# Attention ahead of two MoE layers on one core: another order of the attention stage, and fewer weight conversions in it

## The chip, the cores and the metric

The kernel runs on one core of a Trainium2 chip. The metric is device time in microseconds, from a run's start to its end; the median of several runs counts. The engines are TensorE (PE in the profile, its weight loads PEld), VectorE (DVE), ScalarE (ACT), GpSimd (POOL) and SyncE (SP), whose queue issues all transfers.

## The reference

Random-feature attention, then two feed-forward layers, all in float32.

```python
def phi(x):                                    # x scaled by D ** -0.25
    proj = einsum('bhsd,md->bhsm', x, omega)   # D = 64 -> M = 128 features
    h = proj - sum(x * x) / 2
    return exp(h - max(h, axis=-1)) / sqrt(m)
kv  = einsum('bhsm,bhsd->bhmd', phi(k), v)
z   = sum(phi(k), axis=2)
num = einsum('bhsm,bhmd->bhsd', phi(q), kv)
den = einsum('bhsm,bhm->bhs', phi(q), z) + 1e-6
x   = (num / den) as [2304 tokens, 512]
h = x @ w_in;  x = (h - tanh(h)) @ w_out                 # MoE 1, d_ff 2048
h = x @ w_in;  out = (h * sigmoid(1.702 * h)) @ w_out    # MoE 2
```

There are 4 batches of 8 heads, with 576 positions each.

## The kernel before, in words

**Attention.** Two heads (j = 0, 1) form a pair, and there are 16 pairs. The work of a pair is cut into these pieces, each a function:

- `att_a`: q projection on TensorE, features on the partitions (tiles y0, y1 and two of the four hs banks of PSUM).
- `att_a_copy`: ScalarE copies it to pq in SBUF, four copies; after the two of a head, GpSimd takes the maximum over the 128 features (`partition_all_reduce`, L113) into mq.
- `att_sub`, `att_exp`: VectorE subtracts that maximum (L117), ScalarE takes the exponential (L120), once for each head.
- `att_b`: k projection on TensorE, positions on the partitions (two hs banks; the fifth block of positions goes beside the rest of a q projection). `att_b_max`: four VectorE maxima (L143). `att_b_exp`: ten ScalarE exponentials (L148) into kp.
- `att_c`: product of kp and v with 65 columns a head (64 of v, one of ones) on TensorE (L158), into y0 (y2 for pair 0). `att_c_copy`: ScalarE copies it to kvz.
- `att_d`: product of pq and kvz, 65 columns, on TensorE (L175), three blocks into y2 and two into y3. `att_d_norm`: VectorE divides by the last column (L187 to L189), first the three blocks, then the two, into xt.
- `att_e`: transposes on TensorE (L199). `att_e_hi`: ScalarE rounds them to the short format (L213), `att_e_lo`: VectorE takes the rest (L218), and SP writes both to DRAM, from where the MoE reads them; block 0 of the MoE's input is also kept in SBUF.

**Order.** The order on each engine is the order of the program, which is written out by hand in `period(k)`. In steady state a period issues: second normalisation of pair k-2, transposes of k-2, k-v product of k-1, copies of q projection k, subtraction and exponential for head 1 of k-1, bit operations of a conversion, high and low parts of k-2, `kfeat(k)` (k projection, maxima and exponentials, with subtraction and exponential for head 0 of k between), last step of the conversion, q product of k-1 and its first normalisation. The q projection of the next pair opens the next period.

**Weights.** A weight tile (one of 16 per layer) has two halves, input and output weights. Each half comes as 64-bit numbers into one of two raw buffers (`load_w`, 512 KB) and is converted: `conv1` two ScalarE passes (L243, L245), `conv2` two VectorE bit operations (L249, L251), `conv3` a ScalarE cast into the high part (L261), `conv4` the subtraction for the low part (L265), on VectorE during attention and on GpSimd during MoE. Before, the attention stage converts 15 of the 16 half tiles that the first MoE pass wants, one in each period.

**MoE.** 144 steps, in four passes of 36 (two layers, two halves of d_ff each). A step is `h_mm` (12 matmuls, L292), an elementwise chain on ScalarE, VectorE and GpSimd (`elem1`, `elem2`), and `y_mm` (12 matmuls, L339 or L343), which runs three steps behind (LAG). In a pass each block of 512 tokens takes 8 steps, one for each weight tile. `conv_mid` puts conversions behind the elementwise chain: conv1 and conv2 of a new half tile, conv3 and conv4 of the one of the step before; the variable `room` says in which steps. The end of the attention (`tails`) lies between the first three MoE steps.

Of the kernel before, what the change touches and what calls it, by code (L numbers as in the profile page):

```python
# [9 lines left out]
F32 = mybir.dt.float32  # L10
# [8 lines left out]
B, H, S, D, M = 4, 8, 576, 64, 128  # L19
# [4 lines left out]
FP = NF // 2  # L24
# [11 lines left out]
ORDER = ((0, 1, 2, 3, 4), (4, 0, 1, 2, 3), (0, 1, 4, 2, 3), (3, 0, 1, 2, 4))  # L36
LAG = 3
PASSES = ((0, 0), (0, 1), (1, 0))
NWARM = 2


@with_exitstack
def body(ctx, tc, qT, kT, v, om, w1, w2, out):
# [23 lines left out]
    nc.vector.memset(qb, QB)  # L67
    tb = cp.tile([128, 1], F32, name="tb")
    nc.vector.memset(tb, -THR2)
    warm = ap.tile([128, 512], F32, tag="kp", name="warm", bufs=2)  # L70
    nc.vector.memset(warm, 0.0)

    def pt(tag):
        return ps.tile([128, 512], F32, tag=tag, name=tag, bufs=4 if tag == "hs" else 1)
# [31 lines left out]

    def att_a_copy(i, tiles):
        pq = pqs[i] = ap.tile([128, 2, S], F32, tag="pq", name="pq", bufs=2)
        for j in range(2):
            nc.scalar.copy(out=pq[:, j, 0:512], in_=tiles[j])  # L110
            nc.scalar.copy(out=pq[:, j, 512:S], in_=rest[i][j][:, :S - 512])  # L111
            mqs[i, j] = ap.tile([128, S], F32, tag="mq", name="mq", bufs=2)
            nc.gpsimd.partition_all_reduce(  # L113
                mqs[i, j], pq[:, j, :], channels=128, reduce_op=bass.bass_isa.ReduceOp.max)
# [7 lines left out]

    def att_b(i):
        kt = kin.pop(i)
        b, r = (pt("hs"), pt("hs")), rest.pop(i)
        for st in range(ST):
            s0 = min(st * 128, S - 128)
            for j in range(2):
                p = slice(64 * j, 64 * j + 64)
                dst = b[j][:, s0:s0 + 128] if st < 4 else r[j][:, 128:256]  # L130
                nc.tensor.matmul(dst, kt[p, s0:s0 + 128], omd[p, :], start=True, stop=True)  # L131
        kps[i] = ap.tile([128, 2, ST, M], F32, tag="kp", name="kp", bufs=2)
        mx = ap.tile([128, 2 * ST], F32, tag="mx", name="mx", bufs=2)
        return (*b, *r), mx
# [17 lines left out]

    def att_c(i):
        kp, vt = kps.pop(i), vin.pop(i)
        c = pt("y0" if i else "y2")
        for j in range(2):
            for st in range(ST):
                nc.tensor.matmul(  # L158
                    c[:, j * DV:j * DV + DV], kp[:, j, st, :], vt[:, j, st, :], start=(st == 0), stop=(st == ST - 1))
        return c  # L160
# [67 lines left out]
    late = {}  # L228
    NU = 4 * NF

    def load_w(u):
        if u >= NU:
            return
        i, part = divmod(u, 2)
        src = (w1, w2)[i // NF]
        raws[u] = cv.tile([128, 512, 2], I32, tag="raw", name="raw", bufs=2)
        nc.sync.dma_start(
            out=raws[u], in_=src[i % NF, :, part, :].bitcast(I32).rearrange("p (a b) -> p a b", b=2))
# [5 lines left out]
        top = raws[u].bitcast(U16).rearrange("p a (b h) -> p a b h", h=2)[:, :, 0, 1]  # L244
        nc.scalar.activation(out=raws[u][:, :, 0], in_=top, func=AF.Copy, scale=0.9998 * 2.0 ** -13, bias=-0.4995)  # L245

    def conv2(u):
        z, c = raws[u][:, :, 0], raws[u][:, :, 1]
        nc.vector.scalar_tensor_tensor(  # L249
            out=z, in0=c, scalar=-0x80000000, in1=z, op0=ALU.bitwise_and, op1=ALU.bitwise_or)  # L250
        nc.vector.scalar_tensor_tensor(  # L251
            out=c, in0=c, scalar=3, in1=z, op0=ALU.logical_shift_left, op1=ALU.bitwise_or)

# [135 lines left out]

    oms = ap.tile([128, M], F32, name="oms")  # L390
    nc.sync.dma_start(out=oms, in_=om)
    load_q(0)
    load_k(0)
    load_q(1)
    load_v(0)
    load_k(1)
    load_w(0)
    load_w(1)
    omd = ap.tile([128, M], F32, name="omd")
    nc.vector.tensor_scalar(out=omd, in0=oms, scalar1=SCALE, scalar2=None, op0=ALU.mult)  # L400
    ident = ap.tile([128, 128], F32, name="ident")
    make_identity(nc, ident)
    wpt = pt("y3")
    for i in range(NWARM):
        nc.tensor.matmul(wpt, warm[:, :128], warm, start=True, stop=True)
    nc.vector.tensor_copy(out=warm[:, :1], in_=wpt[:, :1])
    new_x((0, 0, 0))


    cu = [0]  # L410
    eparts = {}

    def qexp(i, j):
        att_sub(i, j)
        att_exp(i, j)

    def kfeat(k):
        tiles, mx = att_b(k)
        load_k(k + 2)
        for t in (0, 1):  # L420
            att_b_max(tiles, mx, t)
        if k > 1:
            att_sub(k, 0)
        for t in (2, 3):
            att_b_max(tiles, mx, t)
        for t in range(4):
            att_b_exp(k, tiles, mx, t)
        if k > 1:
            att_exp(k, 0)

    att = {}

    cprev, cnext = [], []

    def conv_new(k):
        cprev[:] = []
        if k < N16 - 1:
            cprev.append(cu[0])
            conv1(cu[0])
            cu[0] += 1  # L440

    def period(k):
        if k != 2:
            att[k] = att_a(k)
            load_q(k + 2)
        a = att.pop(k)
        if k == 0:
            att_a_copy(0, a)
            kfeat(0)
            load_v(1)  # L450
            conv_new(0)
            return
        if k == 1:
            att_a_copy(1, a)
            qexp(0, 0)
            kfeat(1)
        else:
            att_d_norm(k - 2, 1)
            if k > 2:
                e = att_e(k - 2)  # L460
        c = att_c(k - 1)
        load_v(k + 1)
        if k == 2:
            e = att_e(0)
        if k == 1:
            att[2] = att_a(2)
            load_q(4)
        if k > 1:
            att_a_copy(k, a)
        qexp(k - 1, 1)  # L470
        if k == 1:
            att_c_copy(0, c)
        old = list(cprev)
        for u in old:
            conv2(u)
        if k > 1:
            parts = att_e_parts(k - 2, e)
            att_e_hi(parts)
            att_c_copy(k - 1, c)
            att_e_lo(k - 2, parts)  # L480
        for u in old:
            conv3(u)
        conv_new(k)
        if k > 1:
            kfeat(k)
        for u in old:
            conv4(u, nc.vector)
            load_w(u + 2)
        if k == 1:
            qexp(1, 0)  # L490
        att_d(k - 1)
        att_d_norm(k - 1, 0)

    for k in range(N16):
        period(k)


    def tail0():
        e = att_e(N16 - 2)
        c = att_c(N16 - 1)  # L500
        att_sub(N16 - 1, 1)
        att_exp(N16 - 1, 1)
        parts = att_e_parts(N16 - 2, e)
        att_e_hi(parts)
        att_e_lo(N16 - 2, parts)
        att_c_copy(N16 - 1, c)

    def tail1():
        att_d(N16 - 1)
# [9 lines left out]


    pend = deque()
    steps = []
    seq = []
    for moe in range(2):
# [5 lines left out]
                          for k, f in enumerate(range(ph * FP, ph * FP + FP, w))]  # L530
    done = set()

    def conv_ok(u):
        i = u // 2
        return u < NU and (i < NF or i - NF in done)

    def do_y():
        (moe, ph, bi), y, ii, g, first, last = pend.popleft()
# [2 lines left out]
            done.update(ii)  # L541
        return (moe, ph, y, bi) if last else None

    def conv_mid(us):
        for u in us:
            conv1(u)
        for u in cprev:
            conv3(u)
            conv4(u, nc.gpsimd)
        for u in us:  # L550
            conv2(u)
        for u in cnext:
            load_w(u + 2)
        cnext[:] = cprev
        cprev[:] = us

    def split_prev():
        if gprev:
            split(gprev.pop())

    att_d_norm(N16 - 2, 1)
    y = None
    gprev = []
    per = len(steps) // 4
    for si, (key, k, fs) in enumerate(steps):
        if si == len(tails):
            early.close()
            late["p"] = pool("late")
        moe, ph, bi = key
        n = BLOCKS[bi][1]  # L570
        ii = [moe * NF + f for f in fs]
        pos = seq.index(key)
        first, last = k == 0, fs[-1] == ph * FP + FP - 1
        h = h_mm(key, [wt[i] for i in ii], n)
        if si < len(tails):
            tails[si]()
        P, sp = divmod(si, per)
        us = []
        room = (sp - 4) * 2 * FP // 28
        if si > 1 and cu[0] < 2 * FP * (P + 1) + min(2 * FP, max(0, room)) and conv_ok(cu[0]):  # L580
            us.append(cu[0])
            cu[0] += 1
        if first:
            y = [pt(f"y{d}") for d in range(ND if moe == 0 else n // 128)]
        ev = do_y() if len(pend) == LAG else None
        if ev:
            evac(*ev, 0)
        g = (elem2 if moe else elem1)(h, us)
        if ev:
            evac(*ev, 1)  # L590
        else:
            evac_split()
        gg = []
        gprev.append((g, gg))
        pend.append((key, y, ii, gg, first, last))
        xk = k - (1 if n == 512 else 0)
        if 0 <= xk < 4 and pos + 1 < len(seq):
            new = seq[pos + 1]
            if (new[0], new[2]) == (moe, bi):
                xblk[new] = xblk[key]  # L600
            else:
                load_x(new, xk)
        if ph and k >= FP // (512 // n) - 2:
            for d in range(2):
                load_part(moe, bi, d + 2 * (last))
    split(gprev.pop())
    while pend:
        ev = do_y()
# [43 lines left out]
```

## Time and profile before

| | us |
|---|---|
| runs shown | 950.32, 946.99, 952.94 (median 950.32) |
| the profiled execution | 947.04 |
| its span | 945.3 |
| TensorE busy in the span | 931.6 |
| ScalarE, VectorE, GpSimd busy | 517.6, 472.9, 444.4 |
| granted TensorE clock, mean | 0.987 |

The attention stage takes the first 145 us of the span, the MoE layers the other 800. Busy time of TensorE is counted from modelled ends of its matmuls, so 99% of the span does not say that it works at its peak. A granted clock of 1.0 is 2.4 GHz, 0.5 is 1.2 GHz.

### The profile page before, as it was taken

Reading aid. Unit: us, or ns where it says so; the run is one execution under the profiler, and the core shown is the slowest. Engines: PE = TensorE matmul, PEld = TensorE weight load, DVE = VectorE, ACT = ScalarE, POOL = GpSimd, SP = SyncE. Lnnn points to the kernel's source line nnn. Section 1 sums busy time; section 2 is a strip of 40 time slices with the busy share of each in tenths; the row PEclk is TensorE's granted clock in tenths of the full one; section 3 lists DMA queues with packets and bytes.
Section 4 is the critical chain, followed back from the end, with each engine's and each line's share of the span. In section 5 each row is a group of like instructions: output and inputs, shape, how many; then the busy total and the mean of one; then the engine's idle time right before and its main releaser. Section 6 shows DMA issues by size and latency. Waiting matters only on the chain.

```text
span 945.3 us, 13443 instructions
## 1 busy us (share of the span) xinstructions
PE 931.6 (99%) x4916; PEld 784.9 (83%) x4916; DVE 472.9 (50%) x717; ACT 517.6 (55%) x1041; POOL 444.4 (47%) x323
## 2 busy tenths in 40 slices
PE   8999999999999999999999999999999999999998
PEld 6888888888888898888888888888888888888887
DVE  4799996566666543666777732323333112121212
ACT  5699997677777655777776733433433221221221
POOL 3355553665656644667786843433334222222221
PEclk7799999999999999999999999999999999999999
DMA  6477764142514134354544543424312133240302
GB/s 215 151 254 234 244 219 154 56 156 89 195 62 144 46 112 134 95 173 156 178 163 152 193 150 112 146 89 156 136 65 89 49 120 120 69 156 12 123 1 90
DMA packets 59890, 124.24 MB, mean 131 GB/s; under 512 B 6704, under 2 KB 11952, under 8 KB 59824
## 3 DMA queue, kind: packets, MB, share of 16 engines
q1 hardware_dynamic: 59824, 123.38, 39.7%
q8 instruction: 39, 0.64, 0.3%
q14 instruction: 27, 0.22, 0.1%
HBM read 90.32 MB, written 33.03 MB: 130 GB/s over the span
## 4 chain that ended last, share of the span: by engine, by line
PE 90%; DVE 6%; DMA 2%; ACT 1%; SPq 1%; issue 0%; ACTq 0%
PE hs L292 41%; PE y L339 20%; PE y L343 20%; PE y L158 4%; DVE mx L143 2%; PE hs L131 2%; PE y L175 1%; DVE xt L189 1%; DVE pq L117 1%; PE y L199 1%; DVE w L265 1%; DMA raw<-w 1%; DMA xb<-ys 1%; DMA xb<-xs 1%; DVE rc L188 0%
## 5 line engine op out<-in xcount | busy, mean ns | idle before, releaser
L292 PE MATMUL hs<-xb,w 128*128 128x512 f32 (+1 forms) x1920 | 419.2, 368 | 1.8 <-DMA xb<-ys 1.0
L292 PEld LDWEIGHTS hs<-xb,w 128*128 128x128 f32 x1920 | 335.5, 189 | 63.4 <-DMA xb<-ys 1.7
L306 POOL TENSOR_TENSOR glo<-wq,ghi 128x512 fp32r<-128x512 f32 x144 | 191.5, 1330 | 398.5 <-ACT ghi L304 398.5
L339 PE MATMUL y<-ghi,w 128*128 128x512 f32 (+1 forms) x640 | 192.3, 368 | 0.0
L326 ACT ACTIVATE wq<-hs 128x512 f32<-128x512 f32 x72 | 43.0, 597 | 269.9 <-PE hs L292 268.5
L343 PE MATMUL y<-w,ghi 128*128 128x512 f32 x576 | 188.6, 389 | 0.0
L327 DVE TENSOR_TENSOR wq<-hs,wq 128x512 f32<-128x512 f32 x72 | 49.6, 689 | 234.2 <-ACT wq L326 234.2
L320 DVE COPY_PREDICATED wq<-m,t 128x512 f32<-128x512 uint16 x72 | 95.5, 1327 | 119.4 <-POOL wq L318 116.0
L339 PEld LDWEIGHTS y<-ghi,w 128*128 128x128 f32 x640 | 116.6, 188 | 20.0
L343 PEld LDWEIGHTS y<-w,ghi 128*128 128x128 f32 x576 | 108.1, 188 | 22.3
L339 PE MATMUL y<-glo,w 128*128 128x512 f32 (+1 forms) x320 | 117.7, 368 | 0.0
L343 PE MATMUL y<-w,glo 128*128 128x512 f32 x288 | 112.1, 389 | 0.0
L113 POOL PARTITION_ALL_REDUCE mq<-pq x32 | 71.7, 2287 | 70.6 <-ACT pq L111 54.2
L318 POOL TENSOR_TENSOR wq<-wq,s 128x512 f32<-128x512 f32 x72 | 93.1, 1294 | 17.8 <-DVE wq L317 17.8
L304 ACT CAST ghi<-wq 128x512 fp32r<-128x512 f32 x144 | 88.1, 612 | 21.9 <-DVE wq L320 21.4
L312 ACT ACTIVATE s<-hs 128x512 f32<-128x512 f32 x72 | 42.9, 596 | 74.8 <-PE hs L292 74.3
L339 PEld LDWEIGHTS y<-glo,w 128*128 128x128 f32 x320 | 60.4, 189 | 10.0
L249 DVE SCALAR_TENSOR_TENSOR raw<-raw 128x512 int32<-128x512 int32 x64 | 60.3, 941 | 12.3 <-ACT raw L245 12.3
L265 POOL TENSOR_TENSOR w<-raw,w 128x512 fp32r<-128x512 f32 x49 | 65.0, 1326 | 1.9 <-ACT w L261 1.9
L343 PEld LDWEIGHTS y<-w,glo 128*128 128x128 f32 x288 | 54.1, 188 | 10.9
L317 DVE SCALAR_TENSOR_TENSOR wq<-wq,hs 128x512 f32<-128x512 f32 x72 | 49.0, 681 | 25.0 <-ACT t L314 24.9
L313 ACT ACTIVATE wq<-s,qb 128x512 f32<-128x512 f32 x72 | 52.2, 725 | 6.6
(64 smaller groups left out, 949.6 us busy)
## 6 DMA issues: line engine op xcount, KB each, us to landing
raw<-w SPq DMA_DIRECT2D x64, 512.0 KB, 4.0
xb<-xs SPq DMA_DIRECT2D x28, 512.0 KB, 4.8
xb<-ys SPq DMA_DIRECT2D x28, 512.0 KB, 4.8
vt<-v SPq DMA_DIRECT2D x16, 325.0 KB, 3.3
qt<-qT SPq DMA_DIRECT2D x16, 288.0 KB, 4.2
kt<-kT SPq DMA_DIRECT2D x16, 288.0 KB, 3.6
op<-ye SPq DMA_DIRECT2D x18, 256.0 KB, 2.1
ye<-op SPq DMA_DIRECT2D x18, 256.0 KB, 6.3
```

The lines of the kernel that those rows point to most:

```text
L113: nc.gpsimd.partition_all_reduce(mqs[i, j], pq[:, j, :], channels=128, reduce_op=bass.bass_isa.ReduceOp.max)
L249: nc.vector.scalar_tensor_tensor(out=z, in0=c, scalar=-0x80000000, in1=z, op0=ALU.bitwise_and, op1=ALU.bitwise_or)
L265: eng.tensor_tensor(out=wt[i][:, part, 1, :], in0=raws.pop(u)[:, :, 1].bitcast(F32), in1=wt[i][:, part, 0, :].bitcast(F32), op=ALU.subtract)
L292: nc.tensor.matmul(h[:, j * n:j * n + n], w[:, 0, a, kt * 128:kt * 128 + 128], x[:, c, kt, :n], start=(k == 0), stop=(k == 11))
L304: nc.scalar.copy(out=hi, in_=g)
L306: nc.gpsimd.tensor_tensor(out=lo, in0=g, in1=hi.bitcast(F32), op=ALU.subtract)
L313: nc.scalar.activation(out=w, in_=s, func=AF.Square, scale=QS, bias=qb)
L318: nc.gpsimd.tensor_tensor(out=w, in0=w, in1=s, op=ALU.mult)
L320: nc.vector.copy_predicated(out=w, mask=m.bitcast(mybir.dt.uint16), data=t)
L327: nc.vector.tensor_tensor(out=s, in0=h, in1=s, op=ALU.mult)
L339: nc.tensor.matmul(y[d][:, :n], w[:, 1, a, d * 128:d * 128 + 128], g[c][:, j * n:j * n + n], **fl)
L343: nc.tensor.matmul(y[d], g[c][:, c0:c0 + 128], w[:, 1, a, :], **fl)
```

## The change

The attention stage is put in another order. The k side (projection, maxima, exponentials) now runs for pair k+1 in period k, so that q projection k and k projection k+1 are adjacent on TensorE; the k-v product of pair k runs in period k instead of k+1, right ahead of the q product of k-1. On VectorE the subtraction for head 0 of pair k comes late in period k, behind low parts and a bit operation. Conversions begin in 8 periods (2, 4, 5, 7, 8, 10, 11, 13) instead of 15, each spread over three periods: conv1, then conv2 and conv3, then conv4. The other eight half tiles of the first pass are converted in MoE steps 1 to 8, input weights of tiles 4 to 7 first (the list US), and the next load is issued at the end of the step that issues conv4, instead of in the next step. The other passes convert within 26 steps instead of 28. At the start k projection 0 comes first, the loads of weights come later, the identity is made in period 0, and a third warm-up matmul stands there.

```diff
-NWARM = 2
+NATT = 8
+US = [*range(NATT), *range(NATT, 2 * FP, 2), *range(NATT + 1, 2 * FP, 2), *range(2 * FP, 4 * NF)]
...
     def att_b(i):
         kt = kin.pop(i)
-        b, r = (pt("hs"), pt("hs")), rest.pop(i)
+        b, r = ((pt("hs"), pt("hs")), rest[i - 1]) if i else ((pt("y2"), pt("y3")), (pt("hs"), pt("hs")))
...
-        c = pt("y0" if i else "y2")
+        c = pt("y0")
...
+    def period(k):
+        old, new, last = cprev[:], [], clast[:]
+        if 1 < k < 14 and k % 3:
+            new.append(ci[0])
+            ci[0] += 1
+        cprev[:] = new
+        clast[:] = old
         if k > 1:
+            att_d_norm(k - 2, 1)
+        if k > 0:
+            att_sub(k - 1, 1)
+            att_exp(k - 1, 1)
+        for x in last:
+            conv4(US[x], nc.vector)
+        for x in old:
+            conv2a(US[x])
+        a = att_a(k)
+        load_q(k + 2)
+        if k + 1 < N16:
+            tiles, mx = att_b(k + 1)
+            load_k(k + 3)
+        att_a_copy(k, a)
+        if k == 0:
+            make_identity(nc, ident)
+            warm_up(1, "y3")
         if k > 1:
+            parts = att_e_parts(k - 2, att_e(k - 2))
+            att_e_hi(parts)
+        if k + 1 < N16:
+            for t in range(4):
+                att_b_max(tiles, mx, t)
+            for t in range(4):
+                att_b_exp(k + 1, tiles, mx, t)
+        if k > 1:
+            att_e_lo(k - 2, parts)
+        c = att_c(k)
+        load_v(k + 2)
+        att_c_copy(k, c)
+        for x in old:
+            conv2b(US[x])
+        att_sub(k, 0)
+        att_exp(k, 0)
+        for x in old:
+            conv3(US[x])
         if k == 1:
+            load_w(0)
+            load_w(1)
+        for x in new:
+            conv1(US[x])
+        if k > 0:
+            att_d(k - 1)
+            att_d_norm(k - 1, 0)
+        for x in last:
+            load_w(x + 2)
+
+    warm_up(2, "y0")
+    tiles, mx = att_b(0)
+    load_k(2)
+    for t in (2, 3, 0, 1):
+        att_b_max(tiles, mx, t)
+    for t in (2, 3, 0, 1):
+        att_b_exp(0, tiles, mx, t)
...
-    def conv_mid(us):
...
+    def conv_mid(xs):
+        for x in xs:
+            conv1(US[x])
+        for x in cprev:
+            conv3(US[x])
+            conv4(US[x], nc.gpsimd)
+        for x in xs:
+            conv2a(US[x])
+            conv2b(US[x])
+        wnext.extend(x + 2 for x in cprev)
+        cprev[:] = xs
...
-        room = (sp - 4) * 2 * FP // 28
-        if si > 1 and cu[0] < 2 * FP * (P + 1) + min(2 * FP, max(0, room)) and conv_ok(cu[0]):
-            us.append(cu[0])
-            cu[0] += 1
+        if P == 0 and sp <= 2 * FP - NATT:
+            room = NATT - 2 * FP + sp
+        else:
+            room = min(2 * FP, max(0, (sp - (9 if P == 0 else 4)) * 2 * FP // 26))
+        if ci[0] < 2 * FP * (P + 1) + room and conv_ok(ci[0]):
+            us.append(ci[0])
+            ci[0] += 1
...
+        while wnext:
+            load_w(wnext.pop(0))
```

## Rows read from the trace of the kernel before

**Rows 1.** Busy time by stretch: us, busy (count) of each engine, PEclk, DMA share, GB/s.
```profile
11.00:35.00 24.00, 22.84 (x118) 20.21 (x115) 14.35 (x24) 13.82 (x37) 12.90 (x6) 0.51 0.42 139
35.00:145.00 110.00, 106.26 (x963) 91.59 (x963) 105.65 (x224) 98.92 (x288) 58.84 (x26) 1.00 0.73 232
145.00:945.00 800.00, 794.68 (x3798) 669.02 (x3797) 350.26 (x462) 399.27 (x703) 371.94 (x285) 1.00 0.35 116
```

**Rows 2.** Timeline of VectorE, one period: start us, us, engine, line, operation, out<-in, xcount.
```profile
79.57 0.15 DVE L187 TENSOR_SCALAR rc<-y 128x4 f32<-128x4 f32 x1
...
80.31 0.75 DVE L117 TENSOR_TENSOR pq<-pq,mq 128x576 f32<-128x576 f32 x1
80.98 1.63 DVE L249 SCALAR_TENSOR_TENSOR raw<-raw 128x512 int32<-128x512 int32 x1
...
83.25 0.81 DVE L218 TENSOR_TENSOR xl<-y,xh 128x512 fp32r<-128x512 f32 x2
84.19 1.29 DVE L143 TENSOR_REDUCE mx<-hs 128x4 f32<-128x512 f32 x2
...
86.46 0.68 DVE L265 TENSOR_TENSOR w<-raw,w 128x512 fp32r<-128x512 f32 x1
87.06 0.15 DVE L187 TENSOR_SCALAR rc<-y 128x6 f32<-128x6 f32 x1
...
87.95 0.15 DVE L187 TENSOR_SCALAR rc<-y 128x4 f32<-128x4 f32 x1
```

**Rows 3.** Timeline of TensorE, the period in which it did not wait.
```profile
36.88 0.69 PE L104 MATMUL y<-qt,omd 64*128 64x512 f32 x1
...
38.11 0.77 PE L199 MATMUL y<-ident,xt 128*128 128x128 f32 x5
38.74 2.45 PE L158 MATMUL y<-vt,kp 128*128 128x65 f32 x20
41.11 1.16 PE L131 MATMUL hs<-omd,kt 64*128 64x128 f32 x16
...
42.43 2.44 PE L175 MATMUL y<-kvz,pq 128*128 128x65 f32 x20
44.80 0.69 PE L104 MATMUL y<-qt,omd 64*128 64x512 f32 x1
```

**Rows 4.** Timeline of GpSimd and VectorE, opening; GpSimd in the period above.
```profile
11.28 5.89 POOL L113 PARTITION_ALL_REDUCE mq<-pq  x3 [9.77 <-ACT kp L148]
...
13.30 1.73 DVE L117 TENSOR_TENSOR pq<-pq,mq 128x576 f32<-128x576 f32 x1 [4.43 <-POOL mq L113]
...
80.61 4.55 POOL L113 PARTITION_ALL_REDUCE mq<-pq  x2 [3.82 <-ACT pq L111]
```

**Rows 5.** Timeline of ScalarE, the same period.
```profile
79.77 0.64 ACT L110 COPY pq<-y 128x512 f32<-128x512 f32 x1
...
81.09 0.68 ACT L120 ACTIVATE pq<-pq 128x576 f32<-128x576 f32 x1
...
85.08 2.14 ACT L148 ACTIVATE kp<-hs,mx 128x128 f32<-128x128 f32 x8
```

**Rows 6.** Timeline of TensorE, opening; in brackets idle time before it and its releaser.
```profile
1.50 3.48 PE L405 MATMUL y<-warm 128*128 128x512 f32 x4 [1.50 <-DVE warm L71]
...
10.39 0.32 PE L104 MATMUL y<-qt,omd 64*128 64x64 f32 x1 [1.62 <-ACT kp L148]
```

**Rows 7.** Chain of waits where MoE begins: start us, us, engine, tile, line, count.
```profile
145.40 2.82 PE hs L292 x12
...
162.10 2.72 PE y L339 x12
```

**Rows 8.** Tile raw in MoE: durations min/median/max ns, starts; last line its loads.
```profile
L243 ACT ACTIVATE raw<-raw x49: 642/665/680, 162.8 to 718.8; 128x512 f32<-128x512 f32 x49
...
L265 POOL TENSOR_TENSOR w<-raw,w x49: 1298/1316/1667, 169.3 to 725.7; 128x512 fp32r<-128x512 f32 x49
...
DMA to landing us min/median/max: 3.1/3.9/6.1
```

More of the change, by code (lines that the diff above doesn't have):

```diff
@@ L69, in body @@
     nc.vector.memset(tb, -THR2)
-    warm = ap.tile([128, 512], F32, tag="kp", name="warm", bufs=2)
+    warm = ap.tile([128, 512], F32, name="warm")
     nc.vector.memset(warm, 0.0)
@@ L108, in att_a_copy @@
         pq = pqs[i] = ap.tile([128, 2, S], F32, tag="pq", name="pq", bufs=2)
+        r = rest.pop(i)
         for j in range(2):
             nc.scalar.copy(out=pq[:, j, 0:512], in_=tiles[j])
-            nc.scalar.copy(out=pq[:, j, 512:S], in_=rest[i][j][:, :S - 512])
+            nc.scalar.copy(out=pq[:, j, 512:S], in_=r[j][:, :S - 512])
             mqs[i, j] = ap.tile([128, S], F32, tag="mq", name="mq", bufs=2)
@@ L229, in body, with load_w @@
     NU = 4 * NF
-    def load_w(u):
-        if u >= NU:
+    def load_w(ci):
+        if ci >= NU:
             return
+        u = US[ci]
         i, part = divmod(u, 2)
@@ L245, in conv1, with conv2a @@
         nc.scalar.activation(out=raws[u][:, :, 0], in_=top, func=AF.Copy, scale=0.9998 * 2.0 ** -13, bias=-0.4995)
-    def conv2(u):
+    def conv2a(u):
         z, c = raws[u][:, :, 0], raws[u][:, :, 1]
@@ L250, in conv2, with conv2b @@
             out=z, in0=c, scalar=-0x80000000, in1=z, op0=ALU.bitwise_and, op1=ALU.bitwise_or)
+    def conv2b(u):
+        z, c = raws[u][:, :, 0], raws[u][:, :, 1]
         nc.vector.scalar_tensor_tensor(
@@ L391, in body @@
     nc.sync.dma_start(out=oms, in_=om)
+    load_k(0)
     load_q(0)
-    load_k(0)
+    load_k(1)
+    load_v(0)
     load_q(1)
[L395 to L398, printed above, removed]
+    load_v(1)
     omd = ap.tile([128, M], F32, name="omd")
@@ L401, in body @@
     ident = ap.tile([128, 128], F32, name="ident")
[L402 to L406, printed above, removed]
-    new_x((0, 0, 0))
[L410 to L421, printed above, removed]
-        if k > 1:
[L423 to L427, printed above, removed]
-        if k > 1:
-            att_exp(k, 0)
@@ L431, in body @@
[L431 to L439, printed above, removed]
-            cu[0] += 1
[L442 to L452, printed above, removed]
-        if k == 1:
[L454 to L492, printed above, removed]
@@ new lines, in warm_up @@
+    def warm_up(n, tag):
+        w = pt(tag)
+        for i in range(n):
+            nc.tensor.matmul(w, warm[:, :128], warm, start=True, stop=True)
+    new_x((0, 0, 0))
+    ci = [0]
+    cprev, clast = [], []
+    def period(k):
[5 more added lines that the diff above has]
+        clast[:] = old
+        if k > 1:
+            att_d_norm(k - 2, 1)
[15 more added lines that the diff above has]
+            warm_up(1, "y3")
+        if k > 1:
+            parts = att_e_parts(k - 2, att_e(k - 2))
[16 more added lines that the diff above has]
+            conv3(US[x])
+        if k == 1:
+            load_w(0)
[7 more added lines that the diff above has]
+            load_w(x + 2)
@@ L498, in tail0 @@
     def tail0():
-        e = att_e(N16 - 2)
-        c = att_c(N16 - 1)
+        att_d_norm(N16 - 2, 1)
         att_sub(N16 - 1, 1)
         att_exp(N16 - 1, 1)
-        parts = att_e_parts(N16 - 2, e)
+        parts = att_e_parts(N16 - 2, att_e(N16 - 2))
         att_e_hi(parts)
         att_e_lo(N16 - 2, parts)
-        att_c_copy(N16 - 1, c)
     def tail1():
@@ L521, in body @@
     pend = deque()
+    wnext = []
     steps = []
@@ L531, in body, with conv_ok @@
     done = set()
-    def conv_ok(u):
-        i = u // 2
-        return u < NU and (i < NF or i - NF in done)
+    def conv_ok(ci):
+        i = US[ci] // 2 if ci < NU else 0
+        return ci < NU and (i < NF or i - NF in done)
     def do_y():
@@ L542, in do_y @@
         return (moe, ph, y, bi) if last else None
-    def conv_mid(us):
[L545 to L555, printed above, removed]
+    def conv_mid(xs):
[9 more added lines that the diff above has]
+        cprev[:] = xs
     def split_prev():
@@ L559, in split_prev @@
             split(gprev.pop())
-    att_d_norm(N16 - 2, 1)
     y = None
@@ L578, in body @@
         us = []
-        room = (sp - 4) * 2 * FP // 28
-        if si > 1 and cu[0] < 2 * FP * (P + 1) + min(2 * FP, max(0, room)) and conv_ok(cu[0]):
-            us.append(cu[0])
-            cu[0] += 1
+        if P == 0 and sp <= 2 * FP - NATT:
[5 more added lines that the diff above has]
+            ci[0] += 1
         if first:
```

## The prediction

> **What bounds the kernel now.** I read the stretches first, then one period of the attention stage on each engine, then the opening, then the MoE stage. From 35 us to 145 us TensorE shows 106 busy microseconds of 110, VectorE 105.7 and ScalarE 98.9 [rows 1]: three full engines, so the order of the work decides. The VectorE timeline settles which of them closes the ring: from one normalisation at 79.57 to the same one at 87.95 it has no pause over 0.13 us [rows 2]. So a period is VectorE's own list, 8.38 us: second normalisation 0.74, subtraction 0.67, the two bit operations of a conversion 2.27, low parts 0.94, maxima with the other subtraction 2.27, last conversion step 0.60, first normalisation 0.89. In the 2.27 hides a stall. A bit operation of some 0.65 us stood for 1.63, having started 0.37 us after GpSimd's first maximum at 80.61 [rows 2, 4]. The opening shows the same plainly: a subtraction released by the first of three maxima met the second one and took 1.73 us instead of 0.75, while a maximum took 5.89/3 = 1.96 [rows 2, 4]. I read it so: a VectorE operation with both inputs in SBUF that comes while a maximum is in its first 0.98 us waits those out; operations reading PSUM do not.
>
> TensorE is close behind. In the one period that it ran without waiting, from 36.88 to 44.80, its five groups took 7.92 us: q projection 1.23, transposes 0.63, k-v product 2.37, k projection 1.32, q product 2.37 [rows 3]. Before that lie 24 us at half clock [rows 1], which is why the fourth q projection starts only at 36.88. In the MoE stage TensorE has 794.7 busy microseconds of 800 [rows 1]: nothing there can be gained, only lost.
>
> **The change, part by part.** Times here are in the profiled execution, 947.04 us with a span of 945.3; the median of the runs shown is 950.32, 3.3 more, and I come back to that at the end.
>
> *A period.* Let 0 be the start of the second normalisation. VectorE: normalisation to 0.74, subtraction to 1.49 (the next operation can start at 1.41). ScalarE: exponential to 2.20 (0.68 [rows 5]), copies 1.32 [rows 5] to 3.52, high parts 0.68 to 4.2. The first maximum starts 0.84 us after the first copy, as now (79.77 to 80.61 [rows 4, 5]), at 3.04; the second at 5.00, with its first 0.98 us to 5.98. The order that is new puts the subtraction for head 0 between the two maxima, where now both are over: it is released at 5.00 and runs at 5.98. That costs nearly the same 0.98 us which the bit operation loses today; the lock is moved and not removed. With a conversion (both bit operations and last step) VectorE reaches 2.66, maxima 4.26, low parts 5.08, then meets the second maximum: second bit operation 5.98 to 6.63, subtraction to 7.30, first normalisation to 8.19. With bit operations only: low parts wait for the high parts, 4.2 to 5.0, and it ends between 7.98 and 8.19, as the one or the other takes the port first at 5.0; I take 8.1. With the last step alone the subtraction runs from 5.98 and it ends at 7.54. Of 13 full periods (2 to 14) five are of the last kind or lighter, five of the second, three of the first: 5x7.54 + 5x8.1 + 3x8.19 = 102.8. TensorE's 13x7.92 = 103.0 is the same, so I take 103 against 108.5 now, from 36.88 to the first MoE matmul at 145.40 [rows 3, 7]: gain 5.5. Bounds: 13x7.4 = 96, if adjacent projections hide some 0.5 us of weight loading, and 13x8.38 = 109, if VectorE's list stays what it is.
>
> ScalarE's list shortens by the conversions (three passes of 0.665 [rows 8] in 8 periods instead of 15) and stays below 7.9; I cost it at nothing, covered by VectorE. If that cover went, its one exposed wait would be the kvz copy, which now frees y0 for the next q projection. SP's queue: the weight load goes behind the v load, which waits for the k-v product; a conversion starts a full period later, so nothing waits. The q, k and v loads come two periods ahead: nothing.
>
> *The opening.* The two warm-up matmuls end at 4.91 as now [rows 6]. k projection of pair 0 to 6.2, q of 0 to 7.4, k of 1 to 8.7. ScalarE: ten exponentials (8 take 2.14 [rows 5], so 2.6) to 9.3, copies to 10.6, exponentials of pair 1 to 13.1, kvz copy to 13.4, which releases y0: q of 1 from 13.4, k of 2 to 15.9. The second maximum of pair 0 is over at 14.1, its subtraction and exponential at 15.6; the copies then release y0 at 16.1: k-v product of 1 to 18.5, q product of 0 to 20.8. Period 2 starts at 20.8, at full clock throughout. (The identity, moved behind two maxima on GpSimd, is first wanted in period 2: nothing. The third warm-up matmul fills a wait for ScalarE: nothing.)
>
> *The last period* has no k projection: the k-v product waits for the first copy, at 2.8, then 2x2.37: 7.6 us. So the first MoE matmul starts at 20.8+103+7.6 = 131.4 instead of 145.4, and the last k-v product no longer lies between MoE steps (-2.3): 16.3 us gained.
>
> *MoE, steps 1 to 9.* Eight half tiles of the first pass are converted here instead of one, one in each of steps 1 to 8, with two raw buffers. The load of half tile x+2 waits for GpSimd's last step on x; the first ScalarE pass on x+2 waits for the load; ScalarE runs in order, so the cast of x+1 stands behind that pass, and GpSimd's step on x+1 behind the cast. One turn is thus a load (3.1 to 6.1, median 3.9), three ScalarE passes (2.0) and a GpSimd step (1.32) [rows 8], less some 0.25 of overlap between passes: 6.3 to 7.1 us, and 7.8 if the x loads of 0.5 MB in these steps stretch it to 4.8. A step is 2.72+2.72 = 5.44 [rows 7]. I take 7.0, near the median. Half tile 8 is ready some 7.0 us after the last transposes (on ScalarE their high parts 0.68, five passes of the elementwise chain and three of conversions at some 0.62, then GpSimd 1.32); six turns on, half tile 14 at 49. TensorE wants it for the y matmuls of step 6, after 13 groups of 2.72 and two matmuls, at 35.8. So it stands some 13 us; at 6.3 it would be 9, at 7.8 it would be 18. Who waits: y matmuls of steps 4 to 6 for their output weights, h of steps 4 to 7 for their input weights. Later conversions, at most two in three steps, have a free step between load and use: nothing.
>
> *Sum:* 947.0-16.3+13 = 943.7.
>
> **Rivals.**
> (a) *The loop hides.* If loads land in 3.1 us and the product waits overlap, the standstill is 4 us or less and the time 931 to 935. For it: no conversion now makes TensorE wait in MoE. Against it: never today are more than two consecutive steps converting. 0.22.
> (b) *The clock falls in the opening.* Now it fell to half after TensorE stood 1.62 us and stayed there to 35 us [rows 1, 6]. My longest pause is 0.85 us, but beside products of 65 columns. Two projections and two products at half clock cost 1.23+1.32+2.37+2.37 = 7.3 us more: 951. 0.2.
> (c) *Slower: the clock falls in the periods.* The two products of 65 columns now stand adjacent, 4.74 us, where a projection parts them today. In the opening of now TensorE was busy 22.84 of 24 us at half clock without getting the full clock back sooner [rows 1], and no stretch of this trace has the two products side by side, so nothing excludes it. A period wholly at half clock costs up to 7.9 us. It decides from the third such period on (2x7.9 = 15.8 brings 943.7 to 959.5): 960 to 985. [...] 0.1.
> (d) *The lock lasts for the whole maximum.* The subtraction would wait until 6.96 and every period end 0.98 later: 8.94 on average, 13x1.0 = 13 us, 957. The opening speaks against it: 0.98 us of stall beside a maximum of 1.96 [rows 4]. 0.05. This is the rule of the Trainium skill, SBUF — State Buffer, section "SBUF: two separate sides": of a GpSimd operation and a VectorE operation with two SBUF inputs the one that starts first keeps the shared port pair for its whole instruction and the other is blocked. The trace agrees that they block each other and not on how long: 0.98 us of 1.96.
>
> **How the numbers follow.** The forecast, gain in attention mostly given back in the first MoE steps, has 0.43. The predicted time is 943.7; the profiled execution was at the lower end of the runs shown (946.99 to 952.94), so I put the median at 944. The bounds of the terms (periods 96 to 109, standstill 9 to 18) carry the forecast from 933 to 954; with (a) below and (b), (d) above, the range 933 to 957 leaves out (c) and the ends. About 1% is what a measurement of this kernel can tell from no change, here 940.8 to 959.8. Faster: (a) with 0.2 and the lower part of the forecast with 0.12: 0.32. Slower: (c) 0.1 and a tail of (b) and (d) of 0.03: 0.13. Within: 0.55.
>
> **What would show it.** First MoE matmul at 131 (136 or later is (b)); granted clock 1.0 from 5 us to the end; VectorE's subtraction for head 0 at some 1.7 us where conversions run; periods alternating near 7.6 and 8.1; in the first 60 us of MoE, ScalarE idle for raw loads some 2 us in each of six steps, and TensorE idle 13 us there. I am wrong if TensorE has no pause in those steps, if periods exceed 8.38, or if the clock column falls after 20 us.

## The result, and the profile after

The changed kernel takes 942.39 us (median of 6 runs, 942.27 to 943.88) against 951.59 us of the kernel before in the same comparison: ratio 0.9914, 95% interval 0.9889 to 0.9938. The profiled execution took 942.97 us with a span of 941.2. Runs of one kernel differ here by several microseconds with the clock that TensorE was granted, so below the mean clock of a run stands beside its time where it matters.

The stretches of the changed kernel (columns as in [rows 1]):

```profile
11.00:35.00 24.00, 23.05 (x222) 20.70 (x220) 19.03 (x39) 20.28 (x67) 15.40 (x10) 1.00 0.66 202
35.00:130.00 95.00, 92.76 (x873) 82.98 (x873) 89.12 (x190) 81.88 (x246) 49.80 (x25) 1.00 0.68 219
130.00:190.00 60.00, 52.88 (x229) 40.62 (x229) 39.47 (x57) 42.65 (x76) 31.09 (x24) 0.97 0.33 113
190.00:941.00 751.00, 744.10 (x3547) 626.10 (x3546) 326.96 (x416) 366.03 (x642) 350.42 (x268) 1.00 0.35 119
```

Against [rows 1] two things stand out. From 11 to 35 us the clock is 1.00 and no longer 0.51. And from 130 to 190 us, the first MoE steps, TensorE is busy 52.9 of 60 us, so it stands idle 7.1: a pause that was not there before. What the pause costs shows in when the y matmuls of step 0 and of step 8 begin:

```profile
144.35 0.39 PE L346 MATMUL y<-ghi,w 128*128 128x512 f32 x1
...
199.70 0.39 PE L346 MATMUL y<-ghi,w 128*128 128x512 f32 x1
```

They lie 55.35 us apart; eight steps of 5.44 us, as in [rows 7], are 43.5. So the first MoE steps lose 11.8 us: the idle time, and groups that ran longer beside it, some of them at half clock (last section). A period of the attention stage on TensorE, by the starts of its groups, to be held against [rows 3]:

```profile
44.45 0.69 PE L106 MATMUL y<-qt,omd 64*128 64x512 f32 x1
...
45.58 1.11 PE L134 MATMUL hs<-omd,kt 64*128 64x128 f32 x16
...
46.85 0.76 PE L202 MATMUL y<-ident,xt 128*128 128x128 f32 x5
47.45 2.36 PE L161 MATMUL y<-vt,kp 128*128 128x65 f32 x20
49.65 2.40 PE L178 MATMUL y<-kvz,pq 128*128 128x65 f32 x20
51.98 0.69 PE L106 MATMUL y<-qt,omd 64*128 64x512 f32 x1
```

The five groups take 7.53 us from 44.45 to 51.98, not 7.92: q projection 1.13, k projection 1.27, transposes 0.60, the two products 2.20 and 2.33. VectorE in one of the periods with all three conversion parts, to be held against [rows 2]:

```profile
75.78 0.15 DVE L190 TENSOR_SCALAR rc<-y 128x4 f32<-128x4 f32 x1
...
76.52 0.75 DVE L120 TENSOR_TENSOR pq<-pq,mq 128x576 f32<-128x576 f32 x1
77.19 0.68 DVE L272 TENSOR_TENSOR w<-raw,w 128x512 fp32r<-128x512 f32 x1
77.79 0.69 DVE L253 SCALAR_TENSOR_TENSOR raw<-raw 128x512 int32<-128x512 int32 x1
78.39 1.28 DVE L146 TENSOR_REDUCE mx<-hs 128x4 f32<-128x512 f32 x2
...
80.72 1.64 DVE L258 SCALAR_TENSOR_TENSOR raw<-raw 128x512 int32<-128x512 int32 x1
82.28 0.75 DVE L120 TENSOR_TENSOR pq<-pq,mq 128x576 f32<-128x576 f32 x1
...
83.83 0.15 DVE L190 TENSOR_SCALAR rc<-y 128x4 f32<-128x4 f32 x1
```

From one second normalisation (75.78) to the next (83.83) it is 8.05 us, and one operation, the second bit operation at 80.72, took 1.64. In the periods where that operation is absent or comes too early to meet the second maximum, the subtraction for head 0 pays instead; the row answering to [rows 4]:

```profile
24.65 3.91 POOL L116 PARTITION_ALL_REDUCE mq<-pq  x2 [3.60 <-ACT pq L114]
...
26.65 1.71 DVE L120 TENSOR_TENSOR pq<-pq,mq 128x576 f32<-128x576 f32 x1
```

The second of the two maxima starts near 26.6, as they take 1.96 each; the subtraction that the first one releases needs 1.71 instead of 0.75. Two rows of the chain of waits, as in [rows 7]: the first MoE matmul, and 18 us later a raw load that now stands in the chain, where before only TensorE's matmuls stood:

```profile
130.03 2.78 PE hs L299 x12
...
148.51 3.96 DMA raw<-w
```

And the first MoE steps, on ScalarE, GpSimd and TensorE (timeline; in brackets the idle time before an instruction and what ended it):

```profile
152.56 0.67 ACT L247 ACTIVATE raw<-raw 128x512 f32<-128x512 f32 x1 [2.18 <-DMA raw<-w]
...
153.68 0.64 ACT L268 CAST w<-raw 128x512 fp32r<-128x512 f32 x1
...
147.19 1.29 POOL L272 TENSOR_TENSOR w<-raw,w 128x512 fp32r<-128x512 f32 x1
...
154.40 1.30 POOL L272 TENSOR_TENSOR w<-raw,w 128x512 fp32r<-128x512 f32 x1 [1.61 <-ACT w L268]
...
187.63 1.32 POOL L272 TENSOR_TENSOR w<-raw,w 128x512 fp32r<-128x512 f32 x1
...
174.30 0.50 PE L346 MATMUL y<-ghi,w 128*128 128x512 f32 x1 [2.42 <-ACT w L268]
...
175.68 0.74 PE L346 MATMUL y<-ghi,w 128*128 128x512 f32 x2 [0.65 <-POOL w L272]
```

ScalarE stands 2.18 us for a raw load, and the cast of the half tile before (153.68) is behind that pass; GpSimd's last steps on the first seven of the eight half tiles run from 147.19 to 187.63, six turns of 6.74 us on average; TensorE waits 2.42 us for a cast and 0.65 for a low part ahead of the y matmuls of step 4.

### The profile page after: what moved, and what is told of

It is laid out like the page before. It is cut to its first block, busy times and chain, and to the rows that moved or that the text cites. A ratio compares the mean times of both kernels' runs of the same rounds, so it can differ in the third digit from the quotient of the medians.

```text
span 941.2 us, 13426 instructions
## 1 busy us (share of the span) xinstructions
PE 921.3 (98%) x4918; PEld 775.5 (82%) x4918; DVE 478.5 (51%) x709; ACT 515.7 (55%) x1041; POOL 447.0 (47%) x330
## 4 chain that ended last, share of the span: by engine, by line
PE 78%; POOL 6%; DVE 4%; ACT 4%; DMA 3%; issue 3%; SPq 1%; POOLq 0%; ACTq 0%; DVEq 0%
PE hs L299 34%; PE y L350 21%; PE y L346 14%; PE y L178 3%; PE y L161 3%; POOL wq L325 2%; DMA xb<-xs 2%; POOL glo L313 2%; POOL w L272 2%; PE y L106 1%; PE hs L134 1%; DVE wq L327 1%; DVE pq L120 1%; DMA raw<-w 1%; PE y L202 1%
## 5 line engine op out<-in xcount | busy, mean ns | idle before, releaser
L327 DVE COPY_PREDICATED wq<-m,t 128x512 f32<-128x512 uint16 x72 | 99.3, 1379 | 117.2 <-POOL wq L325 115.1
L116 POOL PARTITION_ALL_REDUCE mq<-pq x32 | 64.4, 2059 | 63.7 <-ACT pq L114 60.0
L272 POOL TENSOR_TENSOR w<-raw,w 128x512 fp32r<-128x512 f32 x56 | 74.0, 1321 | 11.3 <-ACT w L268 11.3
```

Of the source, the lines that this page charges most:

```text
L116: nc.gpsimd.partition_all_reduce(mqs[i, j], pq[:, j, :], channels=128, reduce_op=bass.bass_isa.ReduceOp.max)
L272: eng.tensor_tensor(out=wt[i][:, part, 1, :], in0=raws.pop(u)[:, :, 1].bitcast(F32), in1=wt[i][:, part, 0, :].bitcast(F32), op=ALU.subtract)
L327: nc.vector.copy_predicated(out=w, mask=m.bitcast(mybir.dt.uint16), data=t)
```

## The experiments

Each ratio is to runs of the kernel before on the same chip, whose median was 948.89 us beside experiments 1, 4 and 5 and 948.38 us beside the others.

**1. The cast ahead of the pass that waits.**

```diff
-        for x in xs:
-            conv1(US[x])
         for x in cprev:
             conv3(US[x])
             conv4(US[x], nc.gpsimd)
         for x in xs:
+            conv1(US[x])
             conv2a(US[x])
             conv2b(US[x])
```

> The changed kernel, with one edit in the MoE steps: the cast and the last step of the half tile before (conv3, conv4) are issued ahead of the first passes on the new half tile (conv1), so that they no longer stand behind a pass that waits for its load. Theory (two raw buffers and the in-order ScalarE queue make a loop of load, two passes, cast, GpSimd step, 6.7 us a turn against a step of 5.44): the loop now spans two steps, the pause of 13 us in the first MoE steps shrinks to 3 us or less, 931 to 934 us, and GpSimd's last steps on half tiles stand 5.4 to 5.7 us apart. Rival (the steps simply hold too much work for ScalarE and for the port that VectorE and GpSimd share): the pause stays at 9 us or more, 938 us or more, spacing still over 6.3 us.

938.52 us, ratio 0.9886 (0.9858 to 0.9913); 936.65 and 936.72 at clock 1.0, 940.33 and 940.74 at 0.995. Timelines of GpSimd and TensorE in its profiled run (936.65):

```profile
147.39 1.30 POOL L272 TENSOR_TENSOR w<-raw,w 128x512 fp32r<-128x512 f32 x1
...
152.96 1.31 POOL L272 TENSOR_TENSOR w<-raw,w 128x512 fp32r<-128x512 f32 x1
...
187.25 1.30 POOL L272 TENSOR_TENSOR w<-raw,w 128x512 fp32r<-128x512 f32 x1
...
171.33 0.73 PE L346 MATMUL y<-ghi,w 128*128 128x512 f32 x2 [2.19 <-POOL w L272]
```

The spacing fell to (187.25-147.39)/7 = 5.69 us, as the theory said, so the amount of work in a step does not hold it at 6.7. The MoE took 934.9-130.20 = 804.7 us of the span instead of 811.2, 6.5 us less: about half of the pause went, not the three quarters that I expected, and the time lies above the 931 to 934 of the theory. Its largest remainder stands at 171.33, a wait of 2.19 us by the y matmuls of step 4. Their output weights are wanted one group of 2.72 us after the last input weights, while half tiles come 5.7 us apart. So I read the pause as half loop, half a list of half tiles with no slack in its middle; the next experiment gives that slack. A third raw buffer, which would have opened the loop directly, does not fit: the buffers that take the attention's place need 74 KB a partition, and 70.8 would be left. So the two buffers as a link of the loop were not tested by themselves.

**2. Twelve half tiles in the attention stage.**

```diff
-NATT = 8
+NATT = 12
...
-        if 1 < k < 14 and k % 3:
+        if 1 < k < 14:
...
         for x in last:
             conv4(US[x], nc.vector)
+            load_w(x + 2)
...
-        for x in last:
-            load_w(x + 2)
```

> The changed kernel with twelve half tiles converted in the attention stage instead of eight: one begins in each of periods 2 to 13, the weight load is issued right behind the last conversion step, and four are left for MoE steps 1 to 4. Theory (the pause in the first MoE steps is the price of the half tiles that were moved there, and costs more than they save ahead of it): periods with all parts take 8.06 us as the heaviest now do, so the first MoE matmul comes some 3 us later (133), but the pause of 13 us falls to 2 us or less, since these four are wanted two steps later: 932 to 934 us. Rival (eight is the right split: VectorE's list of a period becomes the bound, at 8.4 us or more): first MoE matmul at 137 or later, 938 us or more.

935.81 us, ratio 0.9866 (0.9834 to 0.9897): 933.06 and 933.45 at clock 1.0, 938.17 and 938.24 at 0.994. The profiled run is one of the latter. Its timeline, GpSimd's last steps on the four half tiles and the last k-v product:

```profile
156.11 1.32 POOL L272 TENSOR_TENSOR w<-raw,w 128x512 fp32r<-128x512 f32 x1
...
163.34 1.31 POOL L272 TENSOR_TENSOR w<-raw,w 128x512 fp32r<-128x512 f32 x1 [1.61 <-ACT w L268]
...
169.98 1.32 POOL L272 TENSOR_TENSOR w<-raw,w 128x512 fp32r<-128x512 f32 x1 [1.79 <-ACT w L268]
...
174.79 1.31 POOL L272 TENSOR_TENSOR w<-raw,w 128x512 fp32r<-128x512 f32 x1
...
129.38 3.52 PE L161 MATMUL y<-vt,kp 128*128 128x65 f32 x20 [1.46 <-ACT pq L113]
```

and two stretches of it:

```profile
132.00:136.00 4.00, 4.00 (x21) 4.00 (x20) 1.68 (x4) 0.95 (x2) 1.44 (x1) 0.50 0.26 99
136.00:200.00 64.00, 64.00 (x291) 53.35 (x291) 38.11 (x60) 44.43 (x79) 32.92 (x26) 0.96 0.37 121
```

The loop still turns at 7.23 and 6.64 us, and TensorE is busy 64.00 of 64 us: the same loop, with four half tiles, costs nothing when they are wanted two steps later. The periods with all parts took 8.06 us, ten times in a row. In this run the clock fell to half after TensorE had stood 1.46 us ahead of the last k-v product; the two products and the first MoE group ran at half clock (its first MoE matmul came at 137.16 and took 4.56 us, in experiment 3 at 133.63 and 2.82), which is 5.3 us in all, about the distance to the two runs at clock 1.0.

**3. Twelve, with the cast first.** Both edits.

> The last kernel, with the cast and the last step of the half tile before issued ahead of the first passes of the new one in the MoE steps. Theory: with four half tiles left there is hardly a pause to remove, so the same as with twelve alone, 931 to 934 us. Rival (the pause comes from the order of the passes and not from the number of half tiles): 3 us or more below it.

934.02 us (932.96 to 934.80, all at clock 0.999), ratio 0.9847 (0.983 to 0.9864), the lowest median of this study. The profiled run (934.80) where its MoE begins, in the chain of waits, in TensorE's timeline and as a stretch, and the one wait of TensorE in that stretch:

```profile
133.63 2.82 PE hs L299 x12
```

```profile
128.95 2.45 PE L161 MATMUL y<-vt,kp 128*128 128x65 f32 x20 [1.45 <-ACT pq L113]
```

```profile
133.00:200.00 67.00, 66.61 (x311) 55.40 (x311) 41.00 (x65) 48.59 (x85) 35.38 (x28) 1.00 0.38 128
```

```profile
145.68 0.50 PE L299 MATMUL hs<-xb,w 128*128 128x512 f32 x1 [0.39 <-DVE t L326]
```

At equal clock it stands where the twelve alone stood (933.06, 933.45), as the theory had it: the order of the passes is worth nothing once the half tiles are few. TensorE's 0.39 us of idle time there are a wait for the elementwise chain of an early step: no half tile holds it up any more, so the pause is gone. The MoE takes 933.0-133.63 = 799.4 us.

**4. Without the third warm-up matmul.**

```diff
         if k == 0:
             make_identity(nc, ident)
-            warm_up(1, "y3")
```

> The changed kernel without the third warm-up matmul in period 0. Theory (a TensorE pause of some 2 us between k projection 1 and k-v product 0 is enough to lose the clock, as 1.62 us was in the kernel before): the granted clock falls to half near 11 to 14 us, two projections and two products run at half clock, first MoE matmul at 134 to 140 instead of 130, 946 to 951 us. Rival (the new order is dense enough by itself): clock stays, 942 to 943 us.

952.00 us (944.73 to 956.44, clock 0.987 to 0.994), ratio to the kernel before 1.002 (0.999 to 1.0049). A stretch of its profiled run (947.42), and a row of TensorE's timeline:

```profile
11.00:19.00 8.00, 7.64 (x48) 6.20 (x48) 3.58 (x5) 5.15 (x16) 4.39 (x5) 0.57 0.31 88
```

```profile
10.31 3.29 PE L161 MATMUL y<-vt,kp 128*128 128x65 f32 x20 [1.44 <-ACT pq L113]
```

TensorE stood 1.44 us ahead of k-v product 0, and the clock was at half from about 11 to 18 us; in the changed kernel, below, it stands 0.96 us there, runs the warm-up from 10.27 to 11.23, and the clock holds.

```profile
10.27 1.12 PE L412 MATMUL y<-warm 128*128 128x512 f32 x2 [0.96 <-ACT kp L151]
11.23 2.34 PE L161 MATMUL y<-vt,kp 128*128 128x65 f32 x20
```

In these runs the whole gain of the change hangs on this one matmul. The size I had wrong: the profiled run begins its MoE only 1.8 us later (131.79) and needs 2.5 us more in it, 4.3 of the 8 to 10 us between the medians (952.00 against 942.39, and 943.79 in experiment 6). I had expected the first MoE matmul at 134 or later. Where the other runs, at lower clock still, lose the rest is open; no profile shows one of them.

**5. The kernel before, its first pause filled.**

```diff
         for t, c0, n in ((a, 0, 512), (r, 512, S - 512)):
+            if i == 1 and c0:
+                w = pt("y3")
+                for _ in range(2):
+                    nc.tensor.matmul(w, warm[:, :128], warm, start=True, stop=True)
```

> The kernel before, with two warm-up matmuls put into the TensorE pause of 1.62 us inside q projection 1 (at 8.8 to 10.4 us). Theory (a good part of the gain ahead of the MoE is the clock, which in the kernel before was at half from 11 to 35 us): clock stays at full, q projection 3 starts at 27 to 30 us instead of 36.9, the rest as before, 941 to 945 us. Rival (the gain is the new order; the opening of before waits for ScalarE and VectorE anyway, at either clock): less than 3 us gained, 948 us or more. If the clock falls all the same, the run tells nothing of its price.

945.09 us, ratio 0.9946 (0.9919 to 0.9973), with a wide spread: 938.79 to 941.28 in the four runs at clock 0.996 to 1.0, 943.85 to 948.52 in the six at 0.989 to 0.993. Its profiled run (946.47) is one of the six; a row of TensorE's timeline, and the stretch behind it:

```profile
22.39 3.57 PE L162 MATMUL y<-vt,kp 128*128 128x65 f32 x20 [1.22 <-ACT pq L114]
```

```profile
24.00:28.00 4.00, 4.00 (x25) 3.67 (x26) 2.95 (x4) 1.83 (x5) 2.72 (x2) 0.50 0.24 70
```

The clock survived 10 us and fell after the next pause, 1.22 us ahead of k-v product 1. No profile shows one of the four runs at clock 0.996 to 1.0; they are the shortest of the old order, 1 to 5 us below the medians of the changed kernel.

**6. The kernel before, both pauses filled.** The first edit gives the operand of the small matmuls a buffer of its own, as the changed kernel has it; the first pause is filled as in experiment 5.

```diff
-    warm = ap.tile([128, 512], F32, tag="kp", name="warm", bufs=2)
+    warm = ap.tile([128, 512], F32, name="warm")
...
+        if k == 2:
+            w = pt("y3")
+            for _ in range(2):
+                nc.tensor.matmul(w, warm[:, :128], warm, start=True, stop=True)
         c = att_c(k - 1)
```

> The kernel before, with two warm-up matmuls in the first pause (inside q projection 1) and two more in the second (ahead of k-v product 1, at 21 to 22 us), which the last try left open and where the clock fell in its profile. Theory (the net gain of the change is TensorE's clock in the opening; the new order's gain is given back in MoE): clock at full from 5 us on in most runs, 938 to 941 us, at or below the changed kernel. Rival (the order is worth more than the clock): 944 us or more at full clock.

942.13 us, ratio 0.995 (0.9925 to 0.9975): 941.68, 941.74 and 942.13 at clock 0.999 to 1.0, 945.81 and 946.73 at 0.996 and 0.992. The **changed kernel run again** beside it:

> The changed kernel itself, on the same chip as the other three, to compare with: 942 to 944 us.

It took 943.79 us (942.87 to 945.27), ratio 0.9945 (0.9917 to 0.9973). So the old order with four small matmuls more is level with the whole change. At full clock it stands just above the 938 to 941 that I expected and above those four runs of experiment 5; what the two further matmuls cost is not shown. Stretches of its profiled run (941.68), and the first MoE matmul in its chain:

```profile
11.00:35.00 24.00, 22.10 (x177) 17.58 (x175) 19.77 (x36) 19.62 (x56) 13.49 (x8) 1.00 0.57 183
35.00:145.00 110.00, 106.09 (x956) 91.67 (x956) 104.14 (x222) 97.14 (x280) 56.89 (x25) 1.00 0.71 228
```

```profile
139.46 2.80 PE hs L296 x12
```

Its period is the old one still, 8.38 us, and its clock 1.00 throughout.

## Why the prediction was right

The time (944 forecast, 942.39 measured) and the likeliest case came true, and the terms did too, each within 3 us. In the profiled execution, which the sum was made for, it was 943.7 against 942.97:

| term | predicted, us | measured, us |
|---|---|---|
| q projection of period 2 | 20.8 | 21.59 |
| 13 full periods | 103.0 | 100.6 (21.59 to 122.15) |
| last period | 7.6 | 7.9 |
| first MoE matmul | 131.4 | 130.03 |
| a turn of the conversion loop | 7.0 | 6.74 |
| pause in the first MoE steps | 13 | 11.8 to step 8 |

The whole MoE takes 941.2-130.03 = 811.2 us against 945.3-145.40 = 799.9 before, 11.3 more, although the last k-v product no longer lies in it. In the chain of the kernel before that product took 2.2 us, where I had put 2.3:

```profile
148.77 2.18 PE y L158 x20
```

So the MoE lost 13.5 us, of which 11.8 are the pause. The other 1.7 come behind step 8, and no run says from what.

**The period.** That the lock is moved and not removed was right: the subtraction at 26.65, or the bit operation at 80.72, loses 0.96 us. Two terms were mis-sized. TensorE's own sum, which I took as 7.92, is 7.53, most of the difference in the k-v product (2.37 to 2.20) and the q projection (1.23 to 1.13), and only 0.05 in the k projection that was made adjacent; so the 0.5 us of hidden weight loading in my lower bound is not what the rows show. And VectorE's periods with bit operations alone take 7.82 (29.23 to 37.05, from one second normalisation to the next) and not 8.1, those with all parts 8.05 and not 8.19; the 7.54 of the others was right. TensorE follows them with periods of 7.52, 7.8 and 8.06, 7.74 on average.

**The loop.** Its links were the ones named: load, pass, cast, GpSimd step. My own sum of a turn gives 6.7 with the load of these steps (median 3.6 us instead of 3.9), and my own account of the pause, 7.0 and six turns less 35.8, gives 11.6 with the measured turn: the 11.8 is this mechanism. Experiment 1 cut the link between pass and cast, and the turn went from 6.74 to 5.69; experiment 2 left the loop and removed its price. What I had folded into one number is that half of the pause stays when the loop is cut. (Two slips change nothing: by my terms a turn with a load of 3.1 is 6.2 us, not 6.3, and the average period of rival (d) 8.9, not 8.94.)

**The clock.** Rival (b) did not happen, for a reason that I had costed at nothing: the third warm-up matmul. I wrote that it "fills a wait for ScalarE: nothing"; experiment 4 puts 8 to 10 us on it. (Ahead of it TensorE stood 0.96 us, where my longest pause was 0.85.) The matmul was in the kernel, so this wrong step did not touch the time; that is luck. So is the median. The profiled execution of before lay 3.3 us under its median, and I gave the changed kernel 0.3 without a reason. It came out because its six runs held a clock of 0.998 or 0.999 and lie within 1.6 us, where the runs of the kernel before beside the experiments go from a clock of 0.982 (952.75 to 955.03 us) to 0.989 (946.72 to 949.12).

**A sign of being wrong did come.** I had written that I am wrong if the clock falls after 20 us. It did, from 176 to 180 us, behind the longest wait of the pause (last section), where I had looked for it in the attention stage only. The runs show no price of it: in experiment 6 the one run of the changed kernel at clock 1.0 took 942.97 us and one at 0.998 took 942.87, and in the profile TensorE stood again 9 us later, at 189.00, for a half tile (0.51 us). And TensorE stood idle 7.1 us there, not the 13 that I named as a sign; ScalarE's waits for raw loads were five, of 1.7 to 2.2 us, not six.

**Where the net gain is from** I had not worked out, and here the prediction's story was thin. At full clock the kernel before takes 941.7 us (experiment 6) and begins its MoE at 139.46 instead of 145.40. The new order and the lighter periods bring that to 130.03, 9.4 us more, and the MoE gives back 11.3. So the order and the moved half tiles together are worth nothing at eight half tiles (943.79 against 942.13 on one chip), and by the four runs of experiment 5 at clock 0.996 to 1.0 (938.79 to 941.28) less than nothing; what the change gained is the clock of the opening. With twelve (experiment 3) the new order and the lighter conversions show their worth: 934.02 against 942.13. No run separates the two.

**Rival (c)**, the clock falling beside the two adjacent products, did not happen in the periods, but in one profiled run the clock fell at the end of the stage, where a pause stands ahead of the two (experiment 2). **Rival (d)**: the subtraction at 26.65 met a maximum of 1.96 us and lost 0.96. The Trainium skill, SBUF — State Buffer, section "SBUF: two separate sides", has the holder keep the shared port pair for its whole instruction. The traces differ: in both kernels they show VectorE held up for about the first half of a maximum only (0.96 to 0.98 us of 1.96).

## What to carry to other kernels

Work moved out of a full stage is paid where it lands: before moving it, write down the time at which each piece is wanted there, and the loop of buffers that delivers it; a loop slower than a step was free for four pieces that were wanted late enough, and cost 11.8 us for eight. And before crediting a new order, hold the old one at the same clock: four small matmuls in two pauses gave the old order all that this change gained.

## What the runs showed of the hardware that was not expected

Pauses of TensorE of 1.62, 1.44, 1.22 and 1.46 us (the kernel before, experiments 4, 5 and 2) were followed by half clock; one of 0.96 us with a warm-up matmul right behind was not. The same pause does not always do it: 1.45 us ahead of the last k-v product left the clock at 1.0 in experiment 3, and 1.46 us in experiment 2 did not; 1.21 us at that place left it at 1.0 in the changed kernel. In the kernel before TensorE was busy nearly all the time at half clock for 24 us [rows 1], in experiment 4 for 7, from 11 to 18 us, where q projection 1 and k projection 2 came last before it rose; no run varied that alone. The clock also fell in the MoE pause of the changed kernel, after the waits of 2.42 and 0.65 us; two of its stretches:

```profile
176.00:178.00 2.00, 2.00 (x7) 1.59 (x6) 1.37 (x3) 1.17 (x3) 1.38 (x2) 0.63 0.52 172
178.00:180.00 2.00, 2.00 (x6) 1.51 (x6) 0.76 (x1) 0.70 (x2) 1.14 (x1) 0.52 0.25 98
```
